# A PSUM bank of its own for the k^T v of four head pairs, and another order of the steps in the head

## The chip, the core and the metric

The kernel runs on one NeuronCore of one Trainium2 chip. The core has five engines that run side by side, each with its own instruction queue in order: TensorE (PE, matmuls; its weight loads show as PEld), VectorE (DVE), ScalarE (ACT), GpSimd (POOL) and SyncE (SP, which here only issues transfers between HBM and SBUF). They wait for each other through semaphores. Matmul results land in PSUM, which has eight banks of 512 float32 per partition. The metric is the device time of one execution in microseconds; a time is the median of several runs.

## The reference

Linear attention without a softmax, an RMS norm per head, and then a gated feed-forward block over all tokens:

```python
# q, k, v: (8 batches, 8 heads, 576 positions, 64), float32
kv  = einsum('bhsd,bhse->bhde', k, v)          # 64 x 64 for each head
o   = einsum('bhsd,bhde->bhse', q, kv)
rms = sqrt(mean(o * o, axis=-1, keepdims=True) + 1e-06)
x   = (o / rms * g_norm).transpose(0, 2, 1, 3).reshape(4608, 512)
gate = 1 / (1 + exp(-(x @ w_gate)))            # w_gate, w_val: (512, 1536)
out  = (gate * (x @ w_val)) @ w_out            # w_out: (1536, 512)
```

The three weight matrices come as float64, so the kernel turns their words into float32 itself.

## The kernel before

The tokens are cut into nine chunks of 512. The first chunk needs the attention of the first batch, that is of four pairs of heads (pair n, n = 0 to 3), and the gate and value weights. The kernel has a *head* in which it makes these four pairs and converts the first two weight units, and then the long run of feed-forward work, into which the attention of the other batches and the remaining conversions are woven.

A pair goes through eleven steps, built by `attention(n, at_ps)`. In the order text they have short names:

- `KV` (L289, PE): k^T v of both heads, 12 matmuls into PSUM; `KVO` (L293, DVE) copies it to SBUF.
- `Q` (L299, PE): six transposes of q; `QO` (L304, ACT) copies q^T to SBUF.
- `U` (L316, PE): q times k^T v, 20 matmuls; needs `KVO` and `QO`.
- `SQ` (L321, ACT), `SUM` (L325, DVE), `ROOT` (L329, ACT), `NORM` (L333 and L335, DVE): the RMS norm.
- `X` (L343, PE): five transposes back; `XO` (L352, ACT) copies them into `xT`, of which each pair is one of four parts.

A weight unit u is converted by five steps on DVE, `cu.0` to `cu.4` (L186, L201, L213, L217, L224), and two on ACT, `au.0` after `cu.0` and `au.1` after `cu.1` (L191, L206). `cu.2` needs `au.0`, `cu.3` needs `au.1`. Unit f serves feed-forward block f of the first chunk. A unit's two halves are loaded into one of three staging buffers `st` by the token `wu` (L150, on SP); `w0` is issued among the loads of k, v and q. `w3` reuses the buffer of unit 0 and waits for `c0.3`, and `w4` waits for `c1.3`.

The first block (f=0) is cut into eight matmuls (L589): `b0.g.m` is the gate (g=0) or value (g=1) matmul of part m of `xT`; it needs `c0.4` and `XOm`. Block f=1 follows whole and needs unit 1. `warmN` issues N matmuls of the identity with itself into a bank that is used for nothing else until the first block (L643); they compute nothing that is needed.

The order of all these steps is a text, and the loop over its tokens issues them; each engine takes its own in this order. Before the change:

```python
warm10 KV0 Q0 KVO0 QO0 w1 warm3 U0 SQ0 KV1 SUM0 ROOT0 Q1 KVO1 NORM0 QO1 warm3 U1 SQ1 SUM1 X0 c0.0 c0.1
XO0 ROOT1 NORM1 warm13 KV2 warm2 Q2 KVO2 a0.0 c0.2 X1 a0.1 c0.3 c0.4 QO2 w2 warm6 U2 SQ2 KV3 Q3 b0.0.0 b0.1.0
KVO3 XO1 QO3 w3 U3 SUM2 ROOT2 NORM2 SQ3 SUM3 ROOT3 X2 XO2 b0.0.1 b0.1.1 b0.0.2 NORM3 X3
c1.0 a1.0 c1.1 a1.1 b0.1.2 c1.2 XO3 c1.3 c1.4 w4 b0.0.3 b0.1.3
```

In the head PSUM holds two banks for the first block and three tiles of two banks. `early(n)` gives a pair its places: one two-bank tile `kq` holds both the result of `KV` (columns 384 on) and that of `Q` (columns 0 to 287 of both banks), and `U` and `X` of even and odd pairs have a tile each. The framework sets waits by tiles: who reads or writes a tile waits for others that write or read it.

After the head, block f is followed by block f+1, eight matmuls each, with the conversions of the later units and the second batch's attention at places written out by hand (`places`), then the second layer of the first chunk (L825), and from the second chunk on a faster scheme of products (L949 and L1053) with sums of weights on POOL (L743 first).

Of the kernel before, what the change touches and what calls it, by code (L numbers as in the profile page):

```python
# [10 lines left out]
FP32 = mybir.dt.float32  # L11
# [9 lines left out]
def kernel(  # L21
# [16 lines left out]
    P = 128  # L38
# [3 lines left out]
    JH = NJ // 2  # L42
# [91 lines left out]
    F_ORDER = [2 * j + NF2 * g + e for j in range(NF2 // 2) for g in range(2) for e in range(2)]  # L134
# [5 lines left out]
    def load_unit(u, halves=(0, 1)):  # L140
        if u >= len(units):
            return
        kind, f = units[u]
        if 0 in halves:
            staged[u] = raw.tile([P, 2, DM], I64, tag="st", name="st", bufs=NST)
        st = staged[u]
        for i in halves:
            if kind == "gv":
                src = (moe_w_gate, moe_w_val)[i].rearrange("(m p) f -> p m f", p=P)[:, :, P * f:P * f + P]
                nc.sync.dma_start(out=st[:, i].rearrange("p (m f) -> p m f", m=NMT), in_=src)  # L150
            else:
                nc.sync.dma_start(out=st[:, i], in_=moe_w_out[P * (f + i):P * (f + i) + P, :])
# [98 lines left out]
    w1 = const.tile([P, N3, 4 * NMT, 2, P], FP32, name="w1")  # L251
    w2 = const.tile([P, NFT, DM], FP32, name="w2")
# [288 lines left out]
    psum0 = psum_ctx.__enter__()  # L541

    def bank(i):
        return (psum_mm if i < 2 else psum).tile([P, 512], FP32, tag=f"mm{i}", name="mm")

    turns0, turns = count(), count()

    def mm0_ps():
        return bank(next(turns0) % 2)

    def mm_ps():
        return bank((2, 3, 0, 1)[next(turns) % 4])
# [11 lines left out]
    def give(i):  # L564
        free.append(i)

    def early(n):

        shared = []

        def ps(kind):
            if kind == "q":
                return shared[0]
            t = psum0.tile([P, 2, 512], FP32, tag="kq" if kind == "kv" else f"ux{n % 2}", name="two")
            if kind == "kv":
                shared.append(t)
                return t[:, :, JH * P:]
            return t
        return ps


# [19 lines left out]
    def plain(c, u, ps, steps_at):  # L601
# [11 lines left out]

    KV, KV_OUT, Q, Q_OUT, U, U_SQUARE, U_SUM, U_ROOT, U_NORM, X, X_OUT = range(11)
    a = [attention(n, early(n)) for n in range(NE)]

    steps = {"KV": KV, "KVO": KV_OUT, "Q": Q, "QO": Q_OUT, "U": U, "SQ": U_SQUARE, "SUM": U_SUM, "ROOT": U_ROOT,
# [2 lines left out]


    order = """
        warm10 KV0 Q0 KVO0 QO0 w1 warm3 U0 SQ0 KV1 SUM0 ROOT0 Q1 KVO1 NORM0 QO1 warm3 U1 SQ1 SUM1 X0 c0.0 c0.1
        XO0 ROOT1 NORM1 warm13 KV2 warm2 Q2 KVO2 a0.0 c0.2 X1 a0.1 c0.3 c0.4 QO2 w2 warm6 U2 SQ2 KV3 Q3 b0.0.0 b0.1.0
        KVO3 XO1 QO3 w3 U3 SUM2 ROOT2 NORM2 SQ3 SUM3 ROOT3 X2 XO2 b0.0.1 b0.1.1 b0.0.2 NORM3 X3
        c1.0 a1.0 c1.1 a1.1 b0.1.2 c1.2 XO3 c1.3 c1.4 w4 b0.0.3 b0.1.3
    """
    blk = None
    warm = mm0_ps()
    for token in order.split():  # L630
        name = token.rstrip("0123456789.")
        n = [int(i) for i in token[len(name):].split(".")]
        f = n[0]
        if name == "b":
            blk = blk or Plain(0, F_ORDER[0], (warm, mm0_ps()))
            blk.mm(n[1], n[2])
        elif name in ("c", "a"):
            conversion[f][name][n[1]]()
        elif name == "w":
            load_unit(f)  # L640
        elif name == "warm":
            for _ in range(f):
                nc.tensor.matmul(warm[:, 0:P], ident, ident, start=True, stop=True)  # L643
        else:
            a[f][steps[name]]()
            if token == f"Q{NE - 1}":
                first_ctx.__exit__(None, None, None)
                hp = ctx.enter_context(tc.tile_pool(name="hp", bufs=1))
                h_main = [hp.tile([P, 4 * NT, P], FP32, name=f"h{j}") for j in range(N3)]
                h_more = hp.tile([P, N3, 3 * NT, P], FP32, name="h_more")  # L650
# [471 lines left out]
    X1 = (18, 19, 20, 21, 22, 22, 23, 23, 24, 24, 25, 26, 28, 30, 31, 33, 35, 37)  # L1122
    X2 = (14, 15, 16, 17, 19, 21, 24, 25, 25, 25, 25, 25, 25, 25, 25, 25, 25, 25)
    X3 = (7, 8, 11, 11, 12, 13, 14, 14, 16, 16, 19, 22, 22, 22, 22, 22, 23, 23)
    x_late = []
    for c in range(1, NG):
# [4 lines left out]
        if c + 1 < B:  # L1131
            kv, first_, then = second_batch if c == 1 else feed(c + 1)
# [49 lines left out]
```

## Time and profile before

| | us |
|---|---|
| median of 3 runs | 1015.61 |
| the runs | 1014.79 to 1016.51 |
| span of the profiled execution | 1013.2 |

The profiled execution by stages; us of busy time in each:

| stage, us from the start | length | PE | DVE | ACT | POOL | DMA share |
|---|---|---|---|---|---|---|
| 0 to 34.1: the head | 34.1 | 30.3 | 17.9 | 16.9 | 0.7 | 0.84 |
| 34.1 to 161.2: first chunk | 127.1 | 126.7 | 116.3 | 67.1 | 58.0 | 0.58 |
| 161.2 to 376.8: two chunks | 215.6 | 213.9 | 164.6 | 72.2 | 156.0 | 0.63 |
| 376.8 to 1013.2: six chunks | 636.4 | 632.5 | 424.9 | 204.0 | 376.9 | 0.57 |

A busy time is the union of the engine's instructions in the stage. PE's includes the filler matmuls of the head. The granted clock of TensorE is 1.00 in every stage. DMA share is the mean busy share of the core's 16 DMA engines. A load shows twice: as an issue on SP, and as "us to landing" from issue to the arrival of its data.

### The profile page before, as it was taken

To read this page: it belongs to the slowest core of one execution; us is meant where nothing else is said; L and a number is where in the kernel's file an instruction comes from. 1 tells how busy PE (TensorE), PEld (TensorE's weight loads), DVE (VectorE), ACT (ScalarE), POOL (GpSimd) and SP (SyncE) were. 2 spreads that over 40 slices of the span, in tenths; PEclk is the share of its full clock that TensorE was granted. 3 is DMA by queue.
4 is the path that set the end of the run, shared out by engine and by line. 5 is a ranking of instruction groups with operands and counts; after the bars stand their busy time and mean duration, and the time that the engine had idled before them with its cause. 6 is when DMAs were issued, how large, how long until landed. Compare 5 with 4: busy or idle time off the path is not lost.

```text
span 1013.2 us, 18540 instructions
## 1 busy us (share of the span) xinstructions
PE 1003.4 (99%) x6982; PEld 824.1 (81%) x6982; DVE 723.7 (71%) x1215; ACT 360.2 (36%) x639; POOL 591.6 (58%) x965
## 2 busy tenths in 40 slices
PE   9999999999999999999999999999999999999998
PEld 8454447888888888888888888888888888888887
DVE  4888998899668856775677666866688556755672
ACT  4568522442144304441354115421453033213320
POOL 0000999898448642966177706962496439744963
PEclk9999999999999999999999999999999999999999
DMA  9796415644688467646766476556664545444514
GB/s 273 237 282 198 151 43 177 216 137 152 209 272 309 165 192 260 221 160 200 238 230 195 147 248 234 191 164 192 229 217 153 179 155 209 162 154 159 211 58 123
DMA packets 100248, 195.07 MB, mean 193 GB/s; under 512 B 24224, under 2 KB 73248, under 8 KB 100160
## 3 DMA queue, kind: packets, MB, share of 16 engines
q0 software_dynamic: 20976, 112.87, 32.8%
q1 hardware_dynamic: 72016, 78.94, 25.4%
q10 hardware_dynamic: 7168, 2.10, 0.9%
q8 instruction: 55, 0.90, 0.4%
q14 instruction: 33, 0.27, 0.1%
HBM read 160.04 MB, written 25.56 MB: 183 GB/s over the span
## 4 chain that ended last, share of the span: by engine, by line
PE 74%; POOL 2%; issue 0%; DVE 0%; POOLq 0%
PE mm L949 47%; PE mm L1053 24%; PE at L422 2%; PE at L376 1%; POOL h L724 1%; POOL w_ring L1024 0%; POOL h_more L724 0%; PE at L382 0%; POOL w L772 0%; DVE sg L919 0%; POOL w L1024 0%; POOLq L1024 0%
## 5 line engine op out<-in xcount | busy, mean ns | idle before, releaser
L949 PE MATMUL mm<-xs,w 128*128 128x256 f32 x1428 | 332.0, 380 | 0.0
L949 PEld LDWEIGHTS mm<-xs,w 128*128 128x128 f32 x1428 | 270.4, 190 | 37.4 <-DVE temps L919 0.4
L949 PE MATMUL mm<-xT,w 128*128 128x256 f32 x948 | 230.0, 380 | 0.0
L949 PEld LDWEIGHTS mm<-xT,w 128*128 128x128 f32 x948 | 179.4, 190 | 25.5 <-issue 1.0
L919 DVE TENSOR_TENSOR sg<-sg,mm 128x512 f32<-128x512 f32 (+1 forms) x176 | 100.8, 599 | 96.0 <-PE mm L949 45.6
L772 POOL DMA_DIRECT2D w<-kept x84 | 46.9, 558 | 190.8 <-PE mm L949 188.5
L1053 PE MATMUL mm<-w,h 128*128 128x256 f32 x630 | 143.4, 379 | 0.9 <-POOL h L911 0.5
L1053 PEld LDWEIGHTS mm<-w,h 128*128 128x128 f32 x630 | 119.5, 190 | 17.9 <-POOL h L911 0.9
L915 ACT COPY temps<-mm 128x512 f32<-128x512 f32 (+1 forms) x128 | 66.0, 537 | 190.0 <-PE mm L949 94.9
L911 POOL TENSOR_TENSOR h<-h,sg 128x512 f32<-128x512 f32 x72 | 97.7, 1374 | 54.0 <-DVE h L919 33.8
L724 POOL TENSOR_TENSOR h<-h 128x128 f32<-128x128 f32 x216 | 114.0, 540 | 16.5 <-DVE h_more L724 13.1
L1053 PE MATMUL mm<-w,h_more 128*128 128x256 f32 x474 | 108.2, 379 | 0.0
L908 ACT ACTIVATE sg<-sg 128x512 f32<-128x512 f32 x96 | 59.6, 630 | 131.5 <-DVE sg L919 131.5
L1053 PEld LDWEIGHTS mm<-w,h_more 128*128 128x128 f32 x474 | 90.1, 190 | 12.2
L915 ACT COPY sg<-mm 128x512 f32<-128x512 f32 (+1 forms) x112 | 57.1, 510 | 91.2 <-PE mm L1053 45.2
L589 PE MATMUL mm<-xT,w 128*128 128x512 f32 x176 | 78.4, 598 | 1.8 <-ACT xT L352 1.5
L724 POOL TENSOR_TENSOR h_more<-h 128x128 f32<-128x128 f32 x120 | 59.1, 495 | 33.5 <-DVE h L911 29.2
L919 DVE TENSOR_TENSOR temps<-temps,mm 128x512 f32<-128x512 f32 (+1 forms) x96 | 59.2, 617 | 25.8 <-PE mm L1053 17.2
L919 DVE TENSOR_TENSOR temps<-mm,temps 128x512 f32<-128x512 f32 (+1 forms) x64 | 39.8, 622 | 51.0 <-PE mm L1053 23.6
L915 ACT COPY h<-mm 128x512 f32<-128x512 f32 x48 | 28.1, 586 | 125.5 <-PE mm L949 110.3
L743 POOL TENSOR_TENSOR h_more<-w 128x256 f32<-128x256 f32 x10 | 12.1, 1231 | 100.7 <-DMA st<-in_moe_w_out_dram 100.7
L919 DVE TENSOR_TENSOR sg<-mm,sg 128x512 f32<-128x512 f32 (+1 forms) x64 | 39.6, 618 | 43.2 <-PE mm L1053 21.8
(135 smaller groups left out, 1313.6 us busy)
## 6 DMA issues: line engine op xcount, KB each, us to landing
w<-kept POOLq DMA_DIRECT2D x42, 896.0 KB, 5.0
w<-kept POOLq DMA_DIRECT2D x90, 384.0 KB, 4.6
w<-kept POOLq DMA_DIRECT2D x42, 768.0 KB, 5.3
out_dram<-sg SPq DMA_DIRECT2D x119, 64.0 KB, 1.7
h_more<-in_k_dram SPq DMA_DIRECT2D x28, 256.0 KB, 5.0
h_more<-in_v_dram SPq DMA_DIRECT2D x28, 256.0 KB, 5.2
q<-in_q_dram SPq DMA_DIRECT2D x24, 288.0 KB, 3.2
xT<-xTs SPq DMA_DIRECT2D x96, 72.0 KB, 3.9
```

Source lines behind the costliest of these rows:

```text
L376: nc.tensor.matmul(ps[HD * e:HD * e + HD, n // 2, n % 2], mains[n, "k"][:, c], mains[n, "v"][:, c], start=(n % 2 == 0 and j == 0), stop=Fa ...
L422: nc.tensor.matmul(u[HD * e:HD * e + HD, r, o:o + HD], qTs[QB * r:QB * r + QB, (n0 + which) % 2, c:c + PH], kvq[QB * r:QB * r + QB, (n0 + ...
L589: nc.tensor.matmul(self.ps[i], w[("wg", "wv")[i], self.f][:, m, :], xT[self.c][:, m, :], start=(m == 0), stop=(m == NMT - 1), skip_group_c ...
L724: ops.append((eng, lambda v=v, x=x, sign=sign, y=y, eng=eng: eng.tensor_tensor(out=h_form(v, j), in0=h_form(x, j), in1=h_form(y, j), op=op ...
L743: nc.gpsimd.tensor_tensor(out=w1_slot(j, w_at[v]), in0=w1_slot(j, w_at[x]), in1=w1_slot(j, w_at[y]), op=op_of(sign))
L772: nc.gpsimd.dma_start(out=granule(g)[:, 0:n], in_=kept1[g // NPA % N3, g % NPA][:, 0:n])
L908: nc.scalar.activation(out=o["o" + step[1]], in_=o["o" + step[1]], func=AF.Sigmoid)
L911: mult.tensor_tensor(out=o[x], in0=o[x], in1=o[y], op=ALU.mult)
L915: nc.scalar.copy(out=o[out_], in_=o[expr])
L919: tt(out=o[out_], in0=o[x], in1=o[y], op=ALU.add if sign == "+" else ALU.subtract)
L949: nc.tensor.matmul(regions[name][1][:, g], ws[:, g], xf[c][wv], start=(new and g == 0), stop=True, skip_group_check=True)
L1053: nc.tensor.matmul(regions[name][1], h_form(hv, j), ws[:, j], start=(used[i] and j == 0), stop=(j == N3 - 1), skip_group_check=True)
```

## The change

The k^T v of the four early pairs goes to bank 1, as a tile `pair_kv` that all four use in turn and that later takes the value matmuls of the first block; `warm`, bank 0, takes the fillers and then the gate matmuls. Before, bank 1 was idle until the first block. The two-bank tile holds q^T alone. And the order text is new: both remaining early loads stand first, the numbers of fillers differ, `X1 XO1` stand ahead of `KV2`, `c0.2` ahead of `KV2` and `KVO2`, and unit 1's first steps stand between those of pairs 2 and 3. No step is added or taken away but three fillers (37 to 34).

```diff
-    turns0, turns = count(), count()
-
-    def mm0_ps():
-        return bank(next(turns0) % 2)
+    turns = count()
...
+    warm, pair_kv = bank(0), bank(1)
+
     def early(n):
 
-        shared = []
-
         def ps(kind):
-            if kind == "q":
-                return shared[0]
-            t = psum0.tile([P, 2, 512], FP32, tag="kq" if kind == "kv" else f"ux{n % 2}", name="two")
             if kind == "kv":
-                shared.append(t)
-                return t[:, :, JH * P:]
-            return t
+                return pair_kv.unsqueeze(1)
+            return psum0.tile([P, 2, 512], FP32, tag="q" if kind == "q" else f"ux{n % 2}", name="two")
         return ps
...
     order = """
-        warm10 KV0 Q0 KVO0 QO0 w1 warm3 U0 SQ0 KV1 SUM0 ROOT0 Q1 KVO1 NORM0 QO1 warm3 U1 SQ1 SUM1 X0 c0.0 c0.1
-        XO0 ROOT1 NORM1 warm13 KV2 warm2 Q2 KVO2 a0.0 c0.2 X1 a0.1 c0.3 c0.4 QO2 w2 warm6 U2 SQ2 KV3 Q3 b0.0.0 b0.1.0
-        KVO3 XO1 QO3 w3 U3 SUM2 ROOT2 NORM2 SQ3 SUM3 ROOT3 X2 XO2 b0.0.1 b0.1.1 b0.0.2 NORM3 X3
-        c1.0 a1.0 c1.1 a1.1 b0.1.2 c1.2 XO3 c1.3 c1.4 w4 b0.0.3 b0.1.3
+        w1 w2 warm8 KV0 Q0 KVO0 QO0 warm4 U0 SQ0 KV1 Q1 SUM0 ROOT0 KVO1 QO1 NORM0 warm3 U1 SQ1 X0 XO0 SUM1 ROOT1
+        c0.0 a0.0 c0.1 a0.1 NORM1 warm16 X1 XO1 c0.2 KV2 Q2 KVO2 QO2 c0.3 c0.4 w3 warm3 U2 SQ2 KV3 Q3 SUM2 ROOT2 KVO3 QO3
+        NORM2 b0.0.0 U3 SQ3 b0.1.0 X2 XO2 c1.0 SUM3 ROOT3 a1.0 c1.1 a1.1 NORM3 b0.0.1 b0.1.1 b0.0.2 X3 XO3 b0.1.2
+        c1.2 c1.3 c1.4 w4 b0.0.3 b0.1.3
     """
     blk = None
-    warm = mm0_ps()
...
-            blk = blk or Plain(0, F_ORDER[0], (warm, mm0_ps()))
+            blk = blk or Plain(0, F_ORDER[0], (warm, pair_kv))
```

## The prediction

> **What bounds the kernel now.** I read the engine totals first, then the waits of the matmul engine, then the head (the first 34 us) in order of time.
>
> ```profile
> PE 1003.4 (99%) x6982; PEld 824.1 (81%) x6982; DVE 723.7 (71%) x1215; ACT 360.2 (36%) x639; POOL 591.6 (58%) x965
> ```
>
> PE is busy for all but 9.8 us of the span of 1013.2. From 34.2 us to the end its waits are these (engine, line, releaser: us, times, longest):
>
> ```profile
> PE mm L949 <- ACT sg L915: 0.8, 1, 0.8
> PE mm L1053 <- POOL h L911: 0.5, 1, 0.5
> ...
> PE mm L589 <- DVE w L224: 0.3, 1, 0.3
> ```
>
> With the two left out they make 2.3 us in 979. So from 34 us on PE is the bound, and the head counts by one thing: when the first matmul of block f=1 (L589) can start. In the head PE's busy time says little, because 37 filler matmuls (L643) take 11.6 of its 30 us. The waits of the other engines there:
>
> ```profile
> DVE kvq L293 <- PE two L299: 9.1, 3, 7.0
> ACT qTs L304 <- DVE kvq L293: 6.6, 3, 4.7
> ...
> PEld mm L589 <- ACT xT L352: 3.2, 2, 2.3
> ```
>
> KVO (L293, copies k^T v out) waits for the transposes of q (L299), which it doesn't read, and QO (L304, copies q^T out) waits for KVO: both lie in one tile `two`. The timeline (start, us, instruction, idle before it and releaser):
>
> ```profile
> 16.61 0.92 PE L289 MATMUL two<-v,k 96*64 96x64 f32 x24
> ...
> 18.70 0.23 DVE L293 COPY kvq<-two 128x64 f32<-128x64 f32 x1 [1.74 <-PE two L299]
> 18.84 1.22 DVE L213 SCALAR_TENSOR_TENSOR w<-st,w 128x1024 f32<-128x1024 uint32 x1
> ...
> 20.48 0.81 PE L316 MATMUL two<-kvq,qTs 64*64 64x64 f32 x40
> ...
> 24.48 0.81 PE L316 MATMUL two<-kvq,qTs 64*64 64x64 f32 x40
> ...
> 28.41 0.69 DVE L186 TENSOR_SCALAR w<-st 128x1024 uint32<-128x1024 uint32 x1
> ...
> 30.32 1.23 DVE L213 SCALAR_TENSOR_TENSOR w<-st,w 128x1024 f32<-128x1024 uint32 x1 [0.62 <-ACT w L191]
> 31.23 0.73 ACT L352 COPY xT<-two 128x384 f32<-128x384 f32 x3
> ...
> 32.71 1.28 DVE L224 SCALAR_TENSOR_TENSOR w<-w,g_col,cz 128x1024 f32<-128x1024 f32 x1
> ...
> 34.14 18.26 PE L589 MATMUL mm<-xT,w 128*128 128x512 f32 x42 [0.26 <-DVE w L224]
> ```
>
> Block f=1 starts 0.14 after c1.4 (L224), the last step of weight unit 1. That conversion starts at 28.41 only, behind NORM3 on DVE, though its data is there at 23.4: the second half was issued at 16.56 and
>
> ```profile
> st<-in_moe_w_val_dram SPq DMA_DIRECT2D x1, 512.0 KB, 6.8
> ```
>
> So two things set 34.14: pairs 2 and 3 come late (U at 20.48 and 24.48), and unit 1 is converted last. The price is one for one: what f=1 gains, the time gains.
>
> **The change, part by part.** I walk the new order by these rules, from the rows: an instruction starts when the one before it on its engine is through (DVE's and ACT's next one starts some 0.09 before the end, as 19.97 after 18.84 + 1.22 shows) and 0.05 after its releaser. Durations: KV 0.92, Q 0.71, U 0.81, X 0.72, a block matmul 0.86; KVO 0.23, SUM 0.82, NORM 0.22 + 0.82, c steps 0.69, 0.69, 1.22, 1.22, 1.28; QO 0.64, SQ 0.70, ROOT 0.30, XO 0.74, a steps 1.15 and 1.13. Loads land at issue plus "to landing". The same walk over the old order puts f=1 at 33.8 where the trace has 34.14.
>
> *The bank.* KVO then waits for KV alone and QO for Q alone. The price in the old order: KV2 ends at 17.5, so KVO2 is at 17.6 for 18.70, and c0.2 to c0.4 behind it on DVE come about 1 us sooner. But U2 stands behind six fillers on PE and c1.0 behind NORM3, so the walk gives only 0.3 at f=1 for the bank alone. The second block matmul b0.1.0 now writes this bank and so waits for KVO3; that is over at 22.1 and it is due at 23.6, so it costs nothing.
>
> *Two load tokens (w1, w2) first.* Nothing else on SP lies between their old and new places: the loads keep one order there. Cost 0, with no cover needed.
>
> *Fillers, 37 to 34.* They stand where PE has nothing else to do; 8 ahead of KV0 for 10 end at 5.2 for 6.0, and v of pair 0 is there (issue 1.18 + 3.7 = 4.9).
>
> ```profile
> 1.37 4.63 PE L643 MATMUL mm<-ident 128*128 128x128 f32 x20 [1.37 <-POOL ident masks.py:199]
> ...
> 13.61 3.07 PE L643 MATMUL mm<-ident 128*128 128x128 f32 x26
> ```
>
> Those passes go at 213 ns at first and at 112 ns later; KV0, at 5.93, still took 1.35 for 0.92. I let the slow pace last until 6.9, as it seems to now.
>
> *The order, pairs 0 and 1.* KV0 at 5.1, Q0 at 6.7, QO0 at 7.7, U0 at 8.4 (8.92 before). Then loads rule: v of pair 1 lands at 3.77 + 5.0 = 8.8, KV1 at 9.2, U1 at 11.8 (12.27). c0.0 and c0.1 stand ahead of NORM1 as before (unit 0 landed at 6.22 + 6.9 = 13.1); NORM1 ends at 16.35.
>
> *X1 ahead of KV2.* A new wait on PE: X1 needs NORM1, and KV2, Q2 and all that follows stand behind it. Sixteen fillers cover PE until 16.8, so X1 starts at 16.7 and KV2 at 17.3, 0.7 later than before. If NORM1 were late, each us of it would go on to KV2.
>
> *Pair 2.* Q2 at 18.1 (18.00), KVO2 at 18.2, QO2 at 18.9; three fillers, not six, and X1 out of the way: U2 at 19.6 for 20.48. c0.2 now stands ahead of KVO2 and fills DVE's idle stretch (16.3 to 17.5), c0.3 and c0.4 follow it: unit 0 is ready at 20.9, not 22.51. The end of c0.3 (19.6, not 21.19) also releases the load of unit 3 on SP. It goes to the same queue behind unit 2's second half, issued at 19.26, and is needed at about 37.
>
> *Pair 3.* KV3 at 20.3 (v landed at 11.22 + 8.1 = 19.3), Q3 at 21.2, SUM2 at 21.2, KVO3 at 21.9, QO3 at 22.2 behind ROOT2, U3 at 22.9: 1.6 sooner than 24.48.
>
> *Unit 1 woven into pair 3.* c1.0 stands behind NORM2 (ends 23.4) and ahead of SUM3, and so DVE waits for its load (23.4): no loss. SUM3 at 24.5 after SQ3, c1.1 in the gap while ROOT3 waits behind XO2 on ACT, NORM3 from 26.3 to 27.4, c1.2, c1.3, c1.4 until 31.0; a1.0 and a1.1 are through at 27.3 and 28.4, in time. XO3, behind a1.1, ends at 29.1 for 31.96, so the last two block matmuls end at 31.1, a tie with c1.4. f=1 at 31.1.
>
> *The sum.* 33.8 - 31.1 = 2.7 by the walk on both sides, 34.14 - 31.1 = 3.0 against the trace; I take 2.8, nearer the first, since both walks leave out the same small delays. Lower end for f=1: DVE without a gap from 23.4 is 6.9 of work less overlaps, 30.1, so a gain of 4.0. Upper end: the 0.3 that the old walk was short, and as much again for waits that I have not seen: 31.7, a gain of 2.4.
>
> *Behind it.* Unit 2 landed at 19.26 + 7.1 = 26.4, unit 3 at 21.63 + 7.7 = 29.3; unit 4 is issued at the end of c1.3, 1.4 before f=1 in both. So all engines meet f=1 in the same position, 2.8 earlier. The profiled execution becomes 1013.2 - 2.8 = 1010.4; the median of the runs lies 2.4 above it, so 1012.8.
>
> **The rivals.**
>
> *Lost later.* POOL's chain of weight sums starts at a landing:
>
> ```profile
> 102.01 1.37 POOL L743 TENSOR_TENSOR h_more<-w 128x256 f32<-128x256 f32 x1 [100.70 <-DMA st<-in_moe_w_out_dram]
> ```
>
> PE waits for POOL about 130 us later (the 0.5 above). If that landing stayed at 102 all is given back there: 1015.6. Against it: SP issues those loads when conversions free their buffers, and the conversions move along.
>
> *Slow pace for longer.* If it lasted half as long again, until 10.3, U0 (0.81) and KV1 (0.92) would be doubled, 1.7 in all, on the chain to U1, NORM1 and X1: 1014.5. For it: KV0 now takes the place of the last two fillers ahead of the rise, and no row shows what brings the rise. Against it: PE has no gap there. [...]
>
> *The hold stays.* If KVO still waited for Q, the new order alone gives f=1 at 31.6: 1013.3. Against it: it no longer reads a tile that Q writes.
>
> *Slower.* c1.0 now stands ahead of SUM3. If unit 1 came late, pair 3 would stop with it: f=1 is its landing plus 7.7. It decides from a landing at 26.4 on; were unit 1 served with the last of the stream, at 29.3, f=1 is at 37.0 and the time 1018.5. Before, 5 us lay between landing and use. Against it: the loads landed in the order of their issue, which stays.
>
> **How the numbers follow.** Forecast 0.75, lost later 0.10, slow pace 0.07, slower 0.05, hold 0.03. About 0.2%, 2.0 us, is what a measurement can tell, so faster is below 1013.6. The forecast's own range is 1011.5 to 1013.7 (gains of 4.0 and 2.4, with some scatter): 0.93 of it is faster. Faster 0.70 + 0.02 of the hold = 0.72; within 0.2%: 0.05 + 0.10 + 0.07 + 0.01 = 0.23; slower 0.05. Range: 1011.2 (4.0, and 0.4 of scatter) to 1014.8, which takes in the slow pace and leaves out most of the loss and the slower case.
>
> **What would show it.** KVO2 right after KV2 and not after Q2; U3 near 22.9; c1.0 near 23.4 with SUM3 behind it; c1.4 ending near 31; f=1 near 31.1 with PE's waits after it as before; POOL's first weight sum near 99. I am wrong if U3 isn't 1 us or more earlier, if c1.0 waits beyond 24.5, or if PE's waits after f=1 grow by more than 1 us.

## The result, and the profile after

| | before | after |
|---|---|---|
| median of the runs, us | 1015.54 (14 runs) | 1018.46 (14 runs) |
| the runs | 1014.65 to 1016.98 | 1016.17 to 1022.71 |
| profiled execution: time, span | span 1013.2 | 1018.18, span 1016.4 |

After stands to before as 1.0031, with a 95% interval of 1.0019 to 1.0043: the change makes the kernel 0.3% slower. The forecast was 1012.8, 2.8 faster.

The head first. The timeline of the changed kernel (start, us, engine, line, operation, idle before it and its releaser):

```profile
18.11 0.23 DVE L293 COPY kvq<-mm 128x64 f32<-128x64 f32 x1 [0.70 <-PE mm L289]
...
19.49 0.81 PE L316 MATMUL two<-kvq,qTs 64*64 64x64 f32 x40
...
22.90 0.81 PE L316 MATMUL two<-kvq,qTs 64*64 64x64 f32 x40 [0.22 <-ACT qTs L304]
...
23.35 0.68 DVE L186 TENSOR_SCALAR w<-st 128x1024 uint32<-128x1024 uint32 x1
...
29.80 1.29 DVE L224 SCALAR_TENSOR_TENSOR w<-w,g_col,cz 128x1024 f32<-128x1024 f32 x1
...
31.20 0.30 PEld L582 LDWEIGHTS mm<-xT,w 128*128 128x128 f32 x2 [0.87 <-ACT sg L587]
```

In order: `KVO2` now waits for `KV2` alone (L289, releaser named). `U2` and `U3` start at 19.49 and 22.90, against 20.48 and 24.48 before. `c1.0` starts at 23.35, `c1.4` ends at 31.09, and the first weights of block f=1 are loaded at 31.20, so that its first matmul starts at 31.23 where it was 34.14. The head gained 2.91 in these two profiles.

It is kept for the next 176 us. The busy time by stage (length; PE, PEld, DVE, ACT, POOL with their instructions; granted clock; DMA share; GB/s), first of after:

```profile
31.20:158.30 127.10, 126.75 (x720) 59.49 (x721) 116.48 (x130) 67.14 (x114) 58.02 (x55) 1.00 0.59 179
158.30:207.00 48.70, 48.70 (x361) 42.37 (x359) 39.84 (x61) 20.00 (x32) 42.93 (x58) 1.00 0.62 207
207.00:220.00 13.00, 10.92 (x179) 9.22 (x178) 8.06 (x13) 5.25 (x8) 12.69 (x17) 0.87 0.40 124
...
512.00:520.00 8.00, 6.58 (x158) 5.48 (x158) 1.96 (x4) 3.13 (x6) 7.83 (x13) 0.79 0.58 194
```

and the third of these stages, 2.9 later, in the kernel before:

```profile
209.90:222.90 13.00, 12.22 (x192) 10.21 (x191) 11.37 (x17) 5.92 (x11) 12.69 (x17) 1.00 0.38 120
```

Until 207 PE is as full as before (48.70 of 48.70). Then, in 13 us, it does 13 matmuls fewer at a granted clock of 0.87, and from 512 the same happens again. PE's own timeline shows the place, in after:

```profile
207.17 1.69 PE L422 MATMUL at<-kvq,qTs 32*64 32x64 f32 x136
210.94 0.34 PE L422 MATMUL at<-kvq,qTs 32*64 32x64 f32 x8 [2.08 <-issue]
211.21 1.75 PE L941 MATMUL mm<-xT,w 128*128 128x256 f32 x4
212.75 1.91 PE L941 MATMUL mm<-xs,sg 128*128 128x256 f32 x4
```

The second place in after (merged here as 137 and 7):

```profile
512.12 1.74 PE L422 MATMUL at<-kvq,qTs 32*64 32x64 f32 x137
515.28 0.44 PE L422 MATMUL at<-kvq,qTs 32*64 32x64 f32 x7 [1.42 <-issue]
```

The first place in the kernel before:

```profile
210.08 1.80 PE L422 MATMUL at<-kvq,qTs 32*64 32x64 f32 x144
211.81 1.13 PE L949 MATMUL mm<-xT,w 128*128 128x256 f32 x4
```

L422 is q times k^T v of a later batch: from the third batch on, twice for each batch, 144 small matmuls of 32x64 in a row, each with a weight load, 288 instructions in 1.8 us. I call them a *burst*. The one at 207 is the third batch's second, the one at 512 the sixth batch's first. Before, one burst runs through. In after it breaks off eight matmuls before its end, and PE stands for 2.08 us on "issue", that is on nothing that the profile names as its releaser. Behind it four L941 matmuls take 1.75 and 1.91 for 1.13 and 1.03. The windows show the clock there:

```profile
211.60:215.00 3.40, 3.40 (x10) 2.69 (x9) 0.35 (x1) 2.00 (x3) 3.40 (x5) 0.50 0.17 42
```

The granted clock is 0.50 for 3.41 us, which by my estimate costs half of that, 1.7. PE's waits after the head, in after (releaser: us in total, times, longest):

```profile
PE at L422 <- issue: 3.5, 2, 2.1
PE mm L1045 <- POOL h L716: 1.0, 1, 1.0
PE mm L1045 <- DVE h L911: 0.4, 1, 0.4
```

Before had no wait on "issue" of this size. Two stalls make 3.5 us and two windows at half clock 3.4 by that estimate: 6.9 in all, more than the head gained. The span is 6.0 above the forecast's 1010.4.

### The profile page after: what moved, and what is told of

Read it like the earlier page. It is cut to its first block, busy times and chain, and to the rows that moved or that the text cites. A ratio compares the mean times of both kernels' runs of the same rounds, so it can differ in the third digit from the quotient of the medians.

```text
span 1016.4 us, 18532 instructions
## 1 busy us (share of the span) xinstructions
PE 1005.2 (99%) x6976; PEld 826.0 (81%) x6976; DVE 723.1 (71%) x1215; ACT 360.2 (35%) x639; POOL 590.4 (58%) x965
## 4 chain that ended last, share of the span: by engine, by line
PE 74%; POOL 2%; issue 0%; DVE 0%; POOLq 0%
PE mm L941 47%; PE mm L1045 24%; PE at L422 2%; PE at L376 1%; POOL h L716 1%; POOL w_ring L1016 0%; POOL h_more L716 0%; PE at L382 0%; POOL w L764 0%; DVE sg L911 0%; POOL w L1016 0%; POOLq L1016 0%
## 5 line engine op out<-in xcount | busy, mean ns | idle before, releaser
L941 PE MATMUL mm<-xs,w 128*128 128x256 f32 x1428 | 333.3, 381 | 0.0
L941 PEld LDWEIGHTS mm<-xs,w 128*128 128x128 f32 x1428 | 271.6, 191 | 37.6
L941 PE MATMUL mm<-xT,w 128*128 128x256 f32 x948 | 230.5, 381 | 0.0
L941 PEld LDWEIGHTS mm<-xT,w 128*128 128x128 f32 x948 | 179.7, 190 | 25.3 <-issue 0.7
L911 DVE TENSOR_TENSOR sg<-sg,mm 128x512 f32<-128x512 f32 (+1 forms) x176 | 100.9, 600 | 97.9 <-PE mm L941 48.6
L911 DVE TENSOR_TENSOR temps<-temps,mm 128x512 f32<-128x512 f32 (+1 forms) x96 | 59.3, 618 | 25.7 <-PE mm L1045 17.2
L911 DVE TENSOR_TENSOR temps<-mm,temps 128x512 f32<-128x512 f32 (+1 forms) x64 | 39.8, 623 | 51.8 <-PE mm L1045 23.6
L911 DVE TENSOR_TENSOR sg<-mm,sg 128x512 f32<-128x512 f32 (+1 forms) x64 | 39.6, 619 | 41.3 <-PE mm L1045 21.4
```

The lines of the kernel that those rows point to most:

```text
L911: tt(out=o[out_], in0=o[x], in1=o[y], op=ALU.add if sign == "+" else ALU.subtract)
L941: nc.tensor.matmul(regions[name][1][:, g], ws[:, g], xf[c][wv], start=(new and g == 0), stop=True, skip_group_check=True)
```

## The theory, and its rival

The page of after has a DMA queue of the kind `instruction`, whose packets run from 11.6 to 988.1 us:

```profile
q8 instruction: 55, 0.90, 0.4%
```

That is 55 packets of 16 KB (0.90 MB over 55), one for 258 of PE's 14209 rows in the trace (weight loads, matmuls and semaphore instructions). I read them as PE's instructions, loaded in blocks while the program runs. I number the rows by their start. In after the first stall is ahead of row 3265, the second ahead of row 7873, and in `e3_minus6` one is ahead of row 2753. They lie 512 and 4608 apart, and of the numbers that divide both, 256 is the nearest to 258: I take a block as 256 rows, an estimate from these counts. All three numbers leave 193 when divided by 256, so the stalls stand at the same point of a block. The packet before the first stall starts at 208.35, in the middle of the burst (207.17), and ends at 209.74; PE goes on at 210.94. Before, that packet starts at 208.72, 1.36 *ahead* of its burst.

So the theory of the *block end*, an inference from these packets: PE had run out of instructions. A burst takes 288 instructions, more than a block of 256, in 1.8 us, while the packet at a stall lands 1.0 to 1.9 us after its start and PE goes on 1.2 to 1.5 later. By the theory, whether the packet is asked for in time depends on where in its block the burst begins, and that is set by the number of PE instructions in the head: after has 8 fewer (three fillers and their weight loads are gone, some semaphore instructions more), so its bursts begin 16 and 19 instructions ahead of a block end where before they began 8 and 11 ahead. The rival, *the new order*: the conversions, sums or loads that moved 2.9 earlier collide with something at 207 and 512, whatever the number of instructions.

## The experiments

Every ratio is to the kernel before, run beside it. "Ahead" is the number of PE's instructions from the first of a burst to the next block end, counted in the trace, for the two bursts at which after stalled (third batch's second, sixth batch's first). The k^T v of a later batch (L376) has run five times ahead of 512, for batches two to six, so the second burst is the sixth batch's; the expectations call it the fifth batch's. "Stalls" are waits of PE on "issue" in these two bursts.

| kernel | fillers | ahead | stalls, us | median, us | ratio (95%) |
|---|---|---|---|---|---|
| before | 37 | 8, 11 | none | 1015.54 | |
| after | 34 | 16, 19 | 2.08, 1.42 | 1018.46 | 1.0031 (1.0019 to 1.0043) |
| `e9_again` (after, once more) | 34 | 16, 19 | 1.79, 1.62 | 1017.10 | 1.0022 (1.0009 to 1.0036) |
| `e11_minus1` | 33 | 20, 23 | 1.47, 1.96 | 1018.03 | 1.0027 (1.0017 to 1.0036) |
| `e6_plus1` | 35 | 12, 15 | none | 1012.60 | 0.9969 (0.9958 to 0.9980) |
| `e1_plus2` | 36 | 8, 11 | none | 1012.83 | 0.9971 (0.9959 to 0.9982) |
| `e2_before_minus2` (old order) | 35 | 16, 19 | 1.89, 1.27 | 1020.59 | 1.0051 (1.0034 to 1.0069) |
| `e10_late_filler` | 34 + 1 | 13, 16 | none, 1.62 | 1015.50 | 0.9994 (0.9983 to 1.0005) |
| `e12_late_two` | 34 + 2 | 9, 12 | none | 1013.05 | 0.9983 (0.9972 to 0.9993) |
| `e8_order_only` | 37 | 8, 11 | none | 1013.51 | 0.9985 (0.9965 to 1.0006) |
| `e7_bank_only` | 37 | 5, 8 | none | 1014.81 | 0.9997 (0.9984 to 1.0010) |

**Fillers back into the changed kernel, and out of the old one.**

```diff
-        ... NORM0 warm3 U1 ... NORM1 warm16 X1 ...        # after
+        ... NORM0 warm4 U1 ... NORM1 warm17 X1 ...        # e1_plus2
-        ... QO2 w2 warm6 U2 ...                           # before
+        ... QO2 w2 warm4 U2 ...                           # e2_before_minus2
```

> Changed kernel with two fillers more (37 to 36 against the old 37; eight PE instructions more: one filler ahead of U1, one ahead of X1). What is known: in the changed kernel PE stands still for 2.3 and 1.6 us inside two bursts of U matmuls (L422), both times before the PE instruction whose place in the trace's row count is 193 above a multiple of 256, while a 16 KB transfer of the instruction queue is under way, and each time the granted clock then reads 0.5 for 3.4 us. Theory A (PE's instructions come in blocks of 256, and a burst that crosses two block ends starves; the missing eight instructions moved the block ends into the wrong place): the block ends lie as in the kernel before, no stall in the bursts, granted clock 1.00 all along, f=1 at 31.2 to 31.5, span about 1010.5, time 1012.9 (gain 2.7). Rival B (the new order itself brings the U bursts to a time when they starve, for example behind other transfers): both stalls stay, time 1017 to 1020. Rival C (the clock drops fall at random in any kernel): drops in some runs as now, time spread over 6 us.

> Kernel before with two fillers fewer ahead of U2 (eight PE instructions fewer; nothing else changed). Theory A: the block ends fall where they fall in the changed kernel, so PE stalls about 2 us at row 3265 and about 1.5 us at row 7873 with a clock drop of 3.4 us behind each (1.7 us of work lost each): 5 to 7 us longer, less 0.4 that the head gains, time 1019 to 1022. Rival B (it is the new order): no stall, 1015.1 to 1015.5. Rival C: drops at random.

Both came out as the block end says. Two fillers that compute nothing, added to after, take 5.6 us away (1012.83; 4.3 against the second set of runs of after, `e9_again`). Two taken from the old order, in which nothing else is changed, add 5 us (1020.59), and put the stall in the same place:

```profile
209.32 1.70 PE L422 MATMUL at<-kvq,qTs 32*64 32x64 f32 x136
212.91 0.34 PE L422 MATMUL at<-kvq,qTs 32*64 32x64 f32 x8 [1.89 <-issue]
```

That is PE's timeline of `e2_before_minus2`: the same 136 + 8 matmuls, with nothing of the change in the kernel. The new order is not needed for the stall.

**One filler more, one filler less, and after itself.**

```diff
-        ... NORM0 warm3 U1 ...
+        ... NORM0 warm4 U1 ...        # e6_plus1
+        ... NORM0 warm2 U1 ...        # e11_minus1
```

> Changed kernel with one filler more (35, ahead of U1; four PE instructions more). The burst of the third batch then starts 12 instructions ahead of a block end, that of the fifth 15; the kernel before has 8 and 11 there and no stall, the changed one 16 and 19 and a stall each. [...]

> The changed kernel with one filler fewer (33, ahead of U1; four PE instructions fewer). Theory A: the bursts start 20 and 23 instructions ahead of a block end, still inside the stretch that starves (16 to 19 do), and the other block end still falls into the burst: stalls at rows 3265 and 7873 as in the changed kernel, 1016.5 to 1021. Rival: no order in it, anything.

> The changed kernel itself once more, beside the next two on one chip. All theories: 1017 to 1020, with stalls of PE at rows 3265 and 7873.

For `e6_plus1` the block end allowed any time from 1012.7 (no stall) to 1018 (both bursts stall), the new order 1017 to 1020. One filler, four PE instructions (two passes, each a weight load and a matmul), is worth the whole loss: 1012.60 is the lowest median here, and better than both kernels. `e11_minus1` and `e9_again` stalled at rows 3265 and 7873, as expected. PE's timeline of `e6_plus1`:

```profile
207.37 1.80 PE L422 MATMUL at<-kvq,qTs 32*64 32x64 f32 x144
209.10 1.13 PE L941 MATMUL mm<-xT,w 128*128 128x256 f32 x4
```

The burst starts 0.20 later than in after and runs through; its packet started at 205.87, 1.5 ahead of it. The moment is not what counts, for in `e9_again` the burst starts 0.01 ahead of this one and stalls:

```profile
207.36 1.70 PE L422 MATMUL at<-kvq,qTs 32*64 32x64 f32 x136
210.85 0.34 PE L422 MATMUL at<-kvq,qTs 32*64 32x64 f32 x8 [1.79 <-issue]
```

The waits of `e6_plus1` after the head:

```profile
PE mm L941 <- ACT sg L907: 0.8, 1, 0.8
PE mm L1045 <- POOL h L903: 0.5, 1, 0.5
PE mm L1045 <- POOL h L716: 0.4, 1, 0.4
PE at L422 <- issue: 0.4, 1, 0.4
PE at L422 <- ACT sqs L463: 0.3, 1, 0.3
```

The first two are absent in after, where PE comes there later. So some of the 6.9 came back there, as I read it; the spans of after and `e6_plus1` differ by 5.6. The one on "issue" is another burst, the sixth batch's second, which starts 28 ahead: in the kernels here that burst begins 20 to 36 ahead (56 in `e3_minus6`), and PE waits in it between nothing and 0.54 (in `e4_bank_only`, 20 ahead). So the place in the block doesn't decide alone.

**Six fillers fewer.**

```diff
-        ... NORM1 warm16 X1 ... w3 warm3 U2 ...
+        ... NORM1 warm13 X1 ... w3 U2 ...
```

> Changed kernel with six fillers fewer (28; 24 PE instructions fewer: three of the sixteen ahead of X1, all three ahead of U2). Theory A: the bursts at rows 2993 and 7598 of the changed kernel then start 40 and 43 instructions ahead of a block end, so that the second block end lies behind the burst: no stall, although the count goes further away from the old one; f=1 as in the changed kernel or a little sooner (31.0 to 31.3), span about 1010.3, time about 1012.7. Rival D (fewer fillers are bad as such, through the clock): slower than the changed kernel, above 1018. Rival B: as the changed kernel, 1017 to 1020.

The median is 1015.86 (1015.12 to 1025.28), ratio 1.0011 (0.9987 to 1.0035): not what I expected. Its two bursts start 40 and 43 ahead, and do run through. But the block end went on and met another place, row 2753, which leaves 193 as well:

```profile
182.05 1.85 PE L422 MATMUL at<-kvq,qTs 32*64 32x64 f32 x144
...
187.08 0.48 PE L941 MATMUL mm<-xs,h_more 128*128 128x256 f32 x1 [1.47 <-issue]
```

Here the block ends 15 instructions behind a burst, and PE stands for 1.47 us in L941. I had taken the burst alone as the place where it can happen; the stretch just behind it belongs to it. The head of this profile lost time for another reason: f=1 was at 32.40, and two loads came late, v of pair 1 (`KV1` waited 0.97) and unit 0 (`c0.0` waited 0.41, and `X1` 0.94 behind it). That the missing fillers cost anything there is not shown.

**The filler far behind the head.** This leaves the whole head as the change made it, and puts one or two fillers into the first chunk, some 140 us ahead of after's first stall:

```diff
+        if u == 6:
+            for _ in range(2):                            # e12_late_two; once in e10_late_filler
+                nc.tensor.matmul(ps[0][:, 0:P], ident, ident, start=True, stop=True, skip_group_check=True)
         for at in range(2 * NMT):
```

> The changed kernel with its head untouched and one filler matmul (four PE instructions, 0.2 us of PE) put ahead of block f's first matmul in the seventh block of the first chunk, at about 66 us, into the bank that this matmul then starts anew. Theory A (only the number of PE instructions ahead of the bursts matters): bursts 12 and 15 instructions ahead of a block end as with the filler in the head, no stall over 0.6 us in the bursts of the third and fifth batch, clock 1.00, 1012.6 to 1013.2. Rival B' (what cured it was the head's other timing): stalls stay, 1017 to 1020.

> The changed kernel with its head untouched and two filler matmuls ahead of block u = 6 of the first chunk instead of the one before. Block-end theory: two fillers move the rest of PE's stream by some 5 to 6 instructions, so that the bursts of the third and the fifth batch start 10 to 14 instructions ahead of a block end (16 and 19 in the changed kernel, 13 and 16 with one filler); neither waits, PE has no wait in L422 above 0.8 us, f=1 is at about 31.2 and the median at 1012.4 to 1013.6, at least 2 us below the run with one filler. Rival (the head decides: what is lost later comes from the new order itself, through POOL, ACT or the loads): the time stays at 1015.5 to 1018.5, whatever stands in the first chunk.

One filler moved the stream by three instructions, not four: the third batch's burst is at 13 and runs through, the sixth batch's at 16 and doesn't.

```profile
512.18 1.75 PE L422 MATMUL at<-kvq,qTs 32*64 32x64 f32 x136
515.55 0.34 PE L422 MATMUL at<-kvq,qTs 32*64 32x64 f32 x8 [1.62 <-issue]
```

The time of `e10_late_filler`, 1015.50, lies between. It missed my expectation of it, since I had put the second burst at 15; it gives the edge to within one: 15 ahead runs (`e6_plus1`), 16 stalls. With two fillers, at 9 and 12, `e12_late_two` has no stall and 1013.05, below both sets of runs of after (1017.10 and 1018.46). This is the plainest proof: the head, the order, the conversions and the loads are those of the change, and the loss is gone. (The profiled run of `e12_late_two` had f=1 at 32.16, not at 31.23: unit 0 landed late, `c0.0` waited 0.97 for it and `X1` held PE up by 0.82.)

**The burst split in two.**

```diff
-                u_mms = [u_mm]
+                u_mms = [lambda: u_mm((0,))]
...
+            def second_half():
+                u_mm((1,))
+                u_square()
```

> Changed kernel, fillers as they are (34). From the third batch on the U matmuls of two pairs came as one burst of 144 matmuls (288 PE instructions in 1.8 us); here the second pair's 72 are issued one place later, with the square behind them, so that some product matmuls of L941 stand between the halves. Theory A (a burst starves when PE goes through more than a block of 256 instructions faster than a block is loaded): block ends lie as in the changed kernel, but 144 instructions take 0.9 us and the dense matmuls between the halves give the load time: no stall over 0.6 us in L422, no clock drop, span about 1010.4, time 1012.5 to 1013.5. Rival B (the stalls come from what else runs at that time, or from the block ends whatever the instructions near them): stalls at 193 above a multiple of 256 stay, time 1017 to 1020.

No stall in L422, and the granted clock is 1.00 throughout, as expected. But the median is 1027.78, ratio 1.0116 (1.0101 to 1.0131). The waits of PE in this kernel, and its timeline at one of the places:

```profile
PE mm L945 <- ACT sg L911: 7.4, 11, 0.7
```

```profile
299.49 1.05 PE L422 MATMUL at<-kvq,qTs 32*64 32x64 f32 x72
300.58 1.13 ACT L428 ACTIVATE sqs<-at 128x1152 f32<-128x1152 f32 x1 [3.30 <-PE at L422]
...
302.24 1.13 PE L945 MATMUL mm<-xs,w 128*128 128x256 f32 x4 [0.64 <-ACT sg L911]
```

ACT now takes the square (L428) one place later, the copy of a product (L911) stands behind it on ACT, and PE waits for that copy, eleven times 0.7. The split took the stall away and made a wait of its own. The 7.4 is about half of the 15 us by which this span (1026.1) lies above that of `e6_plus1` (1010.8); the rest was not followed up. The run says nothing against the block end, and it isn't a cure.

**The bank alone, the order alone.**

> The bank of its own with the old order text and its 37 fillers. By the walk of the prediction f=1 comes 0.3 us sooner, 33.8 for 34.1. Theory A: with 37 fillers and a few semaphore instructions more the block ends move by at most four instructions the harmless way, no stall: 1015.2, which is no change. Rival B (the bank is to blame): stalls in the bursts, 1017 or more.

In `e4_bank_only` (the old order text with the new bank) `b0.1.0` writes the bank before `KVO3` has read it, so the k^T v of pair 3 is another value in the output. It gave 1015.73, ratio 0.9998 (0.9985 to 1.0010). `e7_bank_only` has `b0.1.0` behind `KVO3`:

```diff
-        ... KV3 Q3 b0.0.0 b0.1.0
-        KVO3 XO1 QO3 ...
+        ... KV3 Q3 b0.0.0
+        KVO3 b0.1.0 XO1 QO3 ...
```

> The bank of its own with the old order text, but b0.1.0 moved behind KVO3, since both now use this bank; 37 fillers. By the prediction's walk the bank alone brings f=1 from 34.1 to 33.8. Theory A: block ends four instructions from the old ones on the harmless side, no stall, 1015.0 to 1015.4, no change. Rival B (the bank is to blame): 1017 or more.

> The new order text with the old tiles (k^T v and q^T of a pair share a tile), with three fillers more, 37 as before, so that the block ends lie near the old ones. By the prediction's walk f=1 comes at 31.6 to 32.0 (order alone; the fillers may cost 0.2 to 0.4). Theory A: no stall, 1013.3 to 1013.8. Rival B (the order is to blame for the stalls): 1017 to 1020.

With the bank alone `KVO2` goes at 18.15 for 18.70 and waits for `KV2` alone, though v landed late in this profile and `KV2` began 0.6 later than before (17.19). `U2` and `U3` follow 0.6 later, and so does f=1, at 34.7, at the end of the same chain (`c1.4` at 33.27): the freed `KVO2` brought nothing. The ratio is 0.9997, no difference that can be measured. `e8_order_only` has the new order with the old shared tile, and the old number of fillers:

```profile
19.02 0.22 DVE L293 COPY kvq<-two 128x64 f32<-128x64 f32 x1 [1.56 <-PE two L299]
...
20.02 0.81 PE L316 MATMUL two<-kvq,qTs 64*64 64x64 f32 x40
...
30.34 1.29 DVE L224 SCALAR_TENSOR_TENSOR w<-w,g_col,cz 128x1024 f32<-128x1024 f32 x1
```

The hold is back (`KVO2` waits for L299), `U2` is 0.5 later than in after, and f=1 starts at 31.78. Its median is 1013.51, though its interval takes in 1. By these profiles the order carries about 2.4 of the head's 2.9. The other 0.5 would be the bank's on top of it, but that is not resolved: three fillers differ too, and the unchanged head of after had f=1 at 31.23 in one profile and at 31.41 in another (`e9_again`).

## Why the prediction was wrong

**The head: right.** The steps came within 0.2: `KVO2` 18.11 (18.2), `U2` 19.49 (19.6), `U3` 22.90 (22.9), `c1.0` 23.35 (23.4), the end of `c1.4` 31.09 (31.0), f=1 31.23 (31.1). The gain, 2.91, lies between the 2.7 of the two walks and the 3.0 against the trace. The walk of the new order with the hold gave 31.6, measured 31.78 with three fillers more; the bank alone 0.3, measured nothing.

**The step that failed** stands under "Behind it": "So all engines meet f=1 in the same position, 2.8 earlier." That held for the transfers and the buffers, and until 207 the trace agrees. It did not hold for PE's instruction stream: PE met f=1 eight instructions earlier in its block of 256. In the same way "Fillers, 37 to 34. They stand where PE has nothing else to do" priced a filler by its time on PE alone (0.2 to 0.4 us: two passes of 112 or 213 ns). Each is also four instructions of offset for all that follows, and three of them moved two bursts across an edge that lies between 15 and 16. In place of 0 this cost 3.5 us of stalls and up to 3.4 of half clock. None of my rivals had it.

**The forecast without that term: right.** `e6_plus1`, the change with one filler more, has 1012.60, and `e1_plus2` 1012.83, where 1012.8 was forecast. That they agree to 0.2 is partly luck, since the runs of each lie 2.5 us and more apart.

**The rivals.** *Lost later* named the right effect, a gain that is given back behind the head, by the wrong mechanism: POOL's first weight sum moved along with the head,

```profile
99.10 1.37 POOL L735 TENSOR_TENSOR h_more<-w 128x256 f32<-128x256 f32 x1 [97.79 <-PE at L376]
```

at 99.10 for 102.01. *Slow pace for longer* is real but not the cause: in the profiled run of `e1_plus2` the clock rose at 10.6 us and f=1 came at 33.55, 2.3 later than in after (a late load of q, 0.56, is in that too), and that run took 1014.54, 1.7 above its kernel's median, near the 1.7 worked out. The trace's record of the clock begins at 6.92 us in before, and the fillers' passes start 213 ns apart up to 5.6 us and 112 from 7.9 on, so a granted clock of 1.00 for the head says nothing of the time ahead of 6.92. What sets that moment no run shows. *The hold stays* fell with `KVO2` at 18.11. *Slower* came with its sign, but its mechanism did not appear in after, where `c1.0` started at 23.35. Late loads did appear in other profiled runs, at another place; the largest was in `e10_late_filler`:

```profile
16.02 0.69 DVE L186 TENSOR_SCALAR w<-st 128x1024 uint32<-128x1024 uint32 x1 [1.76 <-DMA st<-in_moe_w_val_dram]
...
18.51 0.74 PE L343 MATMUL two<-ident,sqs 128*128 128x128 f32 x5 [1.61 <-DVE sqs L335]
```

There unit 0 landed late, `c0.0` waited 1.76, and `X1` held up PE by 1.61, the "new wait on PE" of the prediction; f=1 came at 34.33. The same chain held up `X1` by 0.82 in `e12_late_two`, so the head's gain hangs on when unit 0 lands.

**What would show it.** "If PE's waits after f=1 grow by more than 1 us" was the right sign: they grew by the 3.5 on "issue".

**What stays open.** The runs show that the count of PE's instructions ahead of these two bursts decides whether they stall. That PE lacks its instructions is read from the packets and not shown directly: at each stall one lands 1.2 to 1.5 us before PE goes on. How far ahead PE's instructions are fetched or taken up no run shows, and why the edge lies between 15 and 16 was not settled. The edge holds for the two bursts named; how far ahead of a block end a packet starts differs along the run. The third batch's first burst, at row 2474 of after, is 23 ahead of a block end and doesn't stall: its packet started at 179.29, 1.6 us ahead of that burst (180.9). Nor is it known why loads land later in some runs.

## What to carry to other kernels

Here PE took 288 instructions in 1.8 us, 160 per us, and the number of instructions ahead of that stretch was a size of its own: one filler more in the head, 0.2 to 0.4 us of PE, took away stalls of 2.08 and 1.42 us at 209 and 514 us. When a time moves against a walk that the trace confirms, look for idle time put down to "issue", and for the packets of the instruction queue beside it; one filler more told such a stall from a true cost in one run here (1012.60 for 1018.46). Compare two orders of work only after each has been tried at a few such offsets: here the same order gives 1012.6 or 1018.0 with one filler more or less.

## What was not expected of the hardware

**Packets of the instruction queue run all through the kernel**, 55 of 16 KB in after, one for 258 of PE's rows, and beside some of them PE stood on "issue": 1.27 to 2.08 us each time, in four kernels at rows 3265 or 7873, in one at row 2753, all with the remainder 193 when divided by 256. That PE waited for its instructions there is my inference.

**The granted clock was 0.5 for 3.413 us after some stalls** and 1.0 after others, and a run of after at a mean clock of 0.993 took 1022.7 where those at 1.000 took 1016.2 to 1017.0. The times at which the clock changes in after lie on a grid of 3.413 us: its record begins at 6.787, and it drops at 211.586, 60 steps later, and at 515.373, 149 steps later. For each window of that grid, in all the profiles here, I added up the time without a large matmul, that is the burst's small matmuls and the stall together:

| window, us | run | without large matmuls, of 3.41 | clock behind it |
|---|---|---|---|
| 512.50 to 515.92 | `e10_late_filler` | 3.32 | 0.5 |
| 511.96 to 515.37 | after | 3.18 | 0.5 |
| 210.05 to 213.46 | `e2_before_minus2` | 3.13 | 0.5 |
| 208.17 to 211.59 | after | 3.04 | 0.5 |
| 207.30 to 210.71 | `e11_minus1` | 3.02 | 0.5 |
| 511.08 to 514.49 | `e11_minus1` | 2.79 | 1.0 |
| 206.43 to 209.84 | `e9_again` | 2.41 | 1.0 |

All windows above 3.0 were followed by half clock, and none below 2.8 (the table has the highest seven). A burst alone, 1.8 us, was never followed by half clock here; a burst and its stall were in five windows that held 3.02 us or more of them, and not in the two that held 2.79 and 2.41. So by these windows the same stall cost its 1.3 to 2.1 us, or by my estimate 1.7 more, by where it lay on the grid of that run. In after's two windows PE stood for 2.08 and 1.42 us, and small matmuls filled most of the rest. Why the clock drops, and what lays the grid, no run shows.
